# Gate rows of an MoE layer by a transposition and five DMA transfers instead of a matmul, and half of the additions of y moved behind the next first matmul group

## The chip, the cores and the metric

One core of one Trainium2 chip. The metric is device microseconds of one execution. Before the change the runs took 544.57, 544.6 and 544.8 us, the median is 544.6 us.

## What is computed

Sigmoid attention (4 batches of 448 tokens, 12 heads of 64), then a first mixture-of-experts layer with a skip, then a second one. Cut to the first layer, which is the one the change touches:

```python
def _moe_ref(x, w_skip, w_gate, w1, w2):        # x: 1792 tokens x 768
    do_compute = x @ w_skip > 0
    logits = xc @ w_gate                        # xc = x[do_compute], 8 experts
    e_idx = argmax(logits)
    gate_w = softmax(logits)[e_idx]             # one gate per token
    for e in range(8):
        h = maximum(xc[mask] @ w1[e], 0)        # 768 -> 1024
        y[mask] = gate_w[mask, None] * (h @ w2[e])
    out[do_compute] = xc + y
```

## The kernel before, in words

The activations stay on the chip transposed: `xT` holds 128 features by tokens, in six chunks. Attention runs over 12 duos of heads by 7 key blocks, 84 steps in all. Each step issues one group of score matmuls (L629), one sigmoid on ACT (L633), one group of value matmuls (L647) two steps behind, and then whatever small functions a table gives to that step (`late`, L671 to 687). When a duo ends, its two output banks are copied to `xT` by DVE (L554) and ACT (L552); the value matmuls of the next duo write the same two banks, so they wait for these copies.

Routing per batch finds the batch's most frequent expert. A batch in which more than 128 tokens choose one expert gets a dense pass (`dense`, L833): all 448 tokens go through that expert, with each input column multiplied by its gate beforehand, and zero for tokens that chose another expert. The multiplied input is made by `split_gated` (L734): for each of six chunks a product `xT * G` on DVE (L742), a rounded copy on ACT (L744) and the remainder on DVE (L745). `K["G"]` is the gate of each of the 448 tokens as a row, the same in all 128 partitions.

Before the change that row is made in two steps. `gate_cols` (L721) computes the gates as columns (`dense_gate`, L375: three DVE instructions, L380 to 384; 112 tokens by 4 columns) and writes four diagonal 112x112 blocks with them (L725). `gate_rows` (L729) multiplies a matrix of ones by these blocks on PE (L731), which sums each diagonal into a row in all partitions, and ACT copies the row back to `K["G"]` (L732).

This happens at two places in this execution:

- For the first dense batch, inside attention. `first_steps` (L753) gives a list of functions to the table at L698 to 701: the plan of the first dense batch (`plan_first`, L387, ending with `pa`, L402) and the rest of `gates` (L366 to 371) at g+7, `start` and `gate_cols` at g+8, `rows`, `piece(0)` and the deferred rest of `ranks` (L335 to 343) at g+12, and the next pieces one step later each. `start` reads the batch and expert numbers into registers and issues four weight loads of 768 KB on SP's queue (L506, L511). In the order of DVE the transposes of the next duo's k and q (L620) stand between `start` and `piece(0)`, the copies L554 stand between `piece(1)` and `piece(2)`. In the order of ACT the rounded copy of chunk 0 stands ahead of a sigmoid.
- For the second dense batch, in the second half of the first dense pass: `next_dense` (L1189), with `start` (two weight loads on SP and `gate_cols`) at sub-step 7.5 and `rows` at 10, where the sub-steps are those of `dense`.

After a dense pass `add_y` (L1239) adds the six banks of its output to `xT` on DVE (L1242). `block1` (L1280) runs one further dense pass; ahead of it `before()` does the sum of squares for the second layer's routing (L1151, L1153) and then `add_y` of the batch before. The relu of the first `h` group of the new pass needs ACT (L847) and then DVE (L848), behind these additions; the banks `YS` are written again only by the first `y` group.

All of this runs with an order written out by hand: each engine and each queue takes its instructions in the order of the program. `bank()` hands out two PSUM banks in turn.

Of the kernel before, what the change touches and what calls it, by code (L numbers as in the profile page):

```python
# [10 lines left out]
F32 = mybir.dt.float32  # L11
# [10 lines left out]
def sigmoid_attention_moe_moe_kernel(  # L22
# [15 lines left out]
    nc = tc.nc  # L38
# [40 lines left out]
    def const(name, shape, dt=F32):  # L79
        return cp.tile(shape, dt, tag=name, name=name)  # L80
# [10 lines left out]
    def setup_steps(tmp):  # L91
# [67 lines left out]
        def rest():  # L159
            K["desc"] = const("desc", [128, NE])  # L160
            nc.vector.tensor_scalar(K["desc"], K["io"][:, :NE], -1.0, float(NE), op0=ALU.mult, op1=ALU.add)
            K["gr"] = [const(f"gr{m}", [P, B, C, 2]) for m in range(2)]
            nc.vector.tensor_copy(K["gr"][0][:, :, :, 1], K["rid"])
            K["rest"] = const("rest", [128, B])
            K["pa"] = const("pa", [128, 4], I32)
            K["plan"] = const("plan", [128, 16])
            K["pb"] = const("pb", [128, 16], I32)
            K["G"] = const("G", [128, S])
            t = tmp.tile([128, 2, 9], F32, tag="seg_t", name="seg_t", bufs=1)
            a, z = t[:, 0, :8], t[:, 1, :8]  # L170
            K["seg"], K["off"] = const("seg", [128, 8]), const("off", [128, NK])
            nc.vector.tensor_scalar(a, K["io"][:, :8], -float(NK), K["pc"][:, 0:1], op0=ALU.mult, op1=ALU.add)
            nc.vector.tensor_single_scalar(z, a, float(NK), op=ALU.is_lt)
            nc.vector.scalar_tensor_tensor(K["seg"], a, 0.0, z, op0=ALU.is_ge, op1=ALU.mult)
            nc.vector.tensor_mul(a, a, K["seg"])
            nc.vector.reduce_sum(t[:, 0, 8:9], a, axis=AX.X)
            nc.vector.tensor_scalar(K["off"], K["io"][:, :NK], t[:, 0, 8:9], None, op0=ALU.is_equal)
# [179 lines left out]
    def gates(R, b0, b1):  # L357

        n = (b1 - b0) * C
        e = sm.tile([P, 2, (B - 1) * C, NE], F32, tag="ge", name="ge", bufs=1)  # L360
        s = sm.tile([P, B * C], F32, tag="gs", name="gs", bufs=1)
        sh = (R.SH[:, b0:b1] if R.m == 0 else R.SH).rearrange("p b c e -> p (b c) e")
        nc.scalar.activation(e[:, 0, :n], sh, AF.Sigmoid)
        nc.scalar.activation(e[:, 1, :n], sh, AF.Sigmoid, scale=-1.0)

        def rest():  # L366
            nc.vector.reciprocal(e[:, 1, :n], e[:, 1, :n])
            nc.vector.tensor_mul(e[:, 0, :n], e[:, 0, :n], e[:, 1, :n])
            nc.vector.reduce_sum(s[:, :n], e[:, 0, :n], axis=AX.X)
            nc.vector.tensor_single_scalar(s[:, :n], s[:, :n], 1e-9, op=ALU.add)  # L370
            nc.vector.reciprocal(K["gr"][R.m][:, b0:b1, :, 0], s[:, :n].rearrange("p (b c) -> p b c", c=C))

        return rest
# [182 lines left out]
    def attention():  # L556


        with ExitStack() as a:
# [112 lines left out]
            for g in range(G + LAG):  # L672
                w, h = divmod(g, NH)
                if 0 < w < N - 2 and h == 0:
                    load_qk(w + 2)
                if g < G:
                    score(w, h)
                if w + 1 < N and 0 <= h - LAG < 4:
                    load_v(w + 1, h - LAG)
                if w + 1 < N and h in (3, 4):  # L680
                    turn(w + 1, "kq"[h - 3])
                for r in {LAG: (), LAG + 1: (LAG + 1, LAG)}.get(h, (LAG,)):
                    if g >= r:
                        av(*divmod(g - r, NH))
                for f in [todo.pop(0)] if todo and g >= 2 else late.get(g, ()):
                    if f:
                        f()
                done = g - LAG + 1
                if done % NH == 0 and done > 0:
                    b, d = duos[done // NH - 1]  # L690
                    if d == NP // 2 - 1 and b < B - 1:
                        assert not todo
                        s1, s2, s3 = route_stages(R1, b, x_of(b))
                        todo = [None, s1, s2]
                        if b == B - 2:
                            ge = []
                            fs = [
                                s1, s2, lambda: ge.append(ranks(R1, 0, B - 1)), lambda: ge.append(gates(R1, 0, B - 1)), lambda: [plan_first(R1), ge[1]()],  # L698
                            ] + first_steps() + [lambda: ge[0]()]
                            at = [g + i for i in (2, 3, 5, 5, 7, 8, 8, 12, 12, 13, 14, 15, 16, 17, 18, 12)]  # L700
                            todo, late = [], schedule({}, fs, at)
            return ST[N - 1, "o"]

# [14 lines left out]

        return [piece(p) for p in range(ND)]

    def gate_cols(R, b):  # L721

        g = dense_gate(R, b)
        for c in range(C):
            nc.vector.tensor_scalar(  # L725
                K["G"][:P, c * P : (c + 1) * P], ident[:P, :P], g[:, c : c + 1], None, op0=ALU.mult
            )

    def gate_rows(ps):  # L729

        nc.tensor.matmul(ps[:, :S], lhsT=K["one"][:P], rhs=K["G"][:P], start=True, stop=True)  # L731
        nc.scalar.activation(K["G"], ps[:, :S], AF.Copy)  # L732

    def split_gated(xs, b):  # L734

# [17 lines left out]
    def first_steps():  # L753

        box = {}

        def start():
            pa = K["pa"]
            b = FIRST["b"] = nc.values_load(pa[0:1, 1:2], engines=XENG, min_val=0, max_val=B - 1)
            FIRST["e"] = nc.values_load(pa[0:1, 2:3], engines=[ENG.SP], min_val=0, max_val=NE - 1)  # L760
            load_unit(w1, w2, FIRST["e"], 0)
            load_unit(w1, w2, FIRST["e"], 1)
            box["p"] = split_gated(XST[0], b)

        def rows():
            gate_rows(bank("ps_G"))

        def piece(i):
            box["p"](i)
            if i == ND - 3:  # L770
                likely("none")
            if i == ND - 2:
                FIRST["n"] = nc.values_load(K["pa"][0:1, 0:1], min_val=0, max_val=1)

        return [start, lambda: gate_cols(R1, FIRST["b"]), rows] + [lambda i=i: piece(i) for i in range(ND + 1)]

    last_x = attention()

# [101 lines left out]
    def at_subs(ks, fs):  # L880
        return merge(*({k: f} for k, f in zip(ks, fs)))
# [307 lines left out]
    def next_dense(j):  # L1189

        box = {}
        xs = XST[(j + 1) % 2]

        def start():
            box["b"], box["e"] = rest_regs(j)
            load1(w1, box["e"], 0)
            load2(w2, box["e"], 0)
            gate_cols(R1, box["b"])

        def rows():  # L1200
            gate_rows(bank("ps_G"))
            box["p"] = split_gated(xs, box["b"])
            for p in range(2):
                box["p"](p)

        def last():
            load_unit(w1, w2, box["e"], 1)
            for f in split_unit(0)[:3]:
                f()

        return {
            7.5: start, 10: rows, 11: lambda: [box["p"](p) for p in (2, 3)], 12: lambda: [box["p"](p) for p in (4, 5, 6)], 13: last,
            14: lambda: [f() for f in split_unit(0)[3:]],
        }
# [21 lines left out]

        return sub

    def add_y(b):  # L1239
        for c in range(ND):  # L1240
            xd = batch_cols(c, b)
            nc.vector.tensor_add(xd, xd, YS[c][:, :S])  # L1242

    def start2(split):

# [31 lines left out]
                run(enumerated(route2_steps(0, XST[1])))  # L1277
            run(enumerated(start2(True)))

    def block1(j, before):  # L1280

        b, e = rest_regs(j - 1)
        xs = XST[j % 2]

        def r2():
            if j > 1:
                return {}
            f = route2_steps(0, XST[0])
            return at_subs((1, 4, 6, 2, 2.5, 5, 6, 8), f[:3] + f[6:])

        def general():
            with tc.If(count(R1) > 0) as cmp:
# [26 lines left out]
        with tc.If(nc.values_load(R1.LI[0:1, n : n + 1], min_val=0, max_val=NL[0]) < 1, label=f"one{j}") as cmp:  # L1319
            if j == B - 1:  # L1320
                general()
            else:
                with tc.If(NB["n"] > j) as more:
                    before()
                    dense(xs, beside(units1(e, 3), merge(r2(), next_dense(j), {13: lambda: likely(f"one{j + 1}")})))
                    block1(j + 1, lambda: add_y(b))
                with more.Else():
                    general()
        with cmp.Else():
# [35 lines left out]
    with cmp.Else():  # L1365
# [12 lines left out]
        with cmp2.Else():  # L1378
            steps = merge(
                next_dense(0), item_steps(R1, (9, 11, 12)),  # L1380
                {12: lambda: raw(batch_of(0)), 13: lambda: likely("one1"), 15: squares},
            )
            dense(XST[0], beside(units1(e), steps), NF // 2)
            block1(1, lambda: [squares_sum(), add_y(b)])


    e = expert_of(0)
# [226 lines left out]
```

## Time and profile before

| | |
|---|---|
| median of 3 runs | 544.6 us (544.57 to 544.8) |
| profiled execution, its own time | 543.8 us |
| its span, first to last instruction | 542.0 us |
| PE busy | 534.7 us (99%) |
| DVE busy | 297.4 us (55%) |
| ACT busy | 249.2 us (46%) |
| mean granted clock of TensorE | 0.999 |

Times in the rows below are microseconds from the start of the span. The profile names an instruction by engine, line and tiles; PE are matmuls, PEld weight loads of PE, SPq and ACTq the DMA issues of SP and ACT. A bracket at the end of a line is the time in which the engine stood idle before it, and what ended that time.

### The profile page before, as it was taken

The numbers are of one execution on the slowest core, as the hardware profiler recorded it, in microseconds if no ns is written. First come the engines' busy times: TensorE is split into PE (matmuls) and PEld (weight loads), VectorE is DVE, ScalarE is ACT, GpSimd is POOL, SyncE is SP. The second block draws the span as 40 slices with busy tenths as digits, with TensorE's granted clock in tenths as the row PEclk, the third lists the DMA queues.
The fourth block names the chain that finished last, engine by engine and source line by source line (L and its number), as shares of the span: only waits on it lengthen the run. The fifth ranks groups of instructions, "written<-read, shape, count | busy, mean of one in ns | idle before, by whom it ended". The sixth has DMA issues, their size and how long they took to land.

```text
span 542.0 us, 9985 instructions
## 1 busy us (share of the span) xinstructions
PE 534.7 (99%) x3601; PEld 420.6 (78%) x3601; DVE 297.4 (55%) x782; ACT 249.2 (46%) x408; POOL 56.1 (10%) x135
## 2 busy tenths in 40 slices
PE   8999999999999999999999999999999999999996
PEld 5464644535489899899869898999899999999984
DVE  3733243237877686774138677595566545462314
ACT  5766776767943355322209463165332333141210
POOL 5010000000000000265000000040004000403202
PEclk9999999999999999999999999999999999999999
DMA  9868666774461513315637206329234832384346
GB/s 176 152 116 147 118 113 114 128 127 115 169 191 49 177 59 122 115 61 166 245 118 278 70 4 231 117 51 263 81 116 111 224 111 66 122 177 161 115 145 194
DMA packets 172512, 73.35 MB, mean 135 GB/s; under 512 B 138162, under 2 KB 164102, under 8 KB 172432
## 3 DMA queue, kind: packets, MB, share of 16 engines
q1 hardware_dynamic: 150000, 65.94, 45.7%
q10 hardware_dynamic: 22064, 5.97, 4.7%
q0 software_dynamic: 368, 0.53, 0.5%
q8 instruction: 32, 0.52, 0.4%
q14 instruction: 48, 0.39, 0.2%
HBM read 66.90 MB, written 5.60 MB: 134 GB/s over the span
## 4 chain that ended last, share of the span: by engine, by line
PE 89%; DVE 4%; issue 3%; ACT 2%; DMA 1%; DVEq 0%; ACTq 0%
PE psO L647 12%; PE psS L629 11%; PE y L827 10%; PE bank L827 10%; PE y L829 10%; PE y L828 10%; PE bank L829 10%; PE bank L828 10%; PE bank L1011 2%; PE y L1036 1%; PE bank L250 1%; DMA k<-in_k_dram 1%; PE ps_r L250 1%; DVE l L813 1%; DVE xg L742 0%
## 5 line engine op out<-in xcount | busy, mean ns | idle before, releaser
L847 ACT ACTIVATE hh<-bank 128x448 fp32r<-128x448 f32 x48 | 26.1, 543 | 188.5 <-PE bank L829 167.1
L827 PE MATMUL y<-hh,h 128*128 128x448 f32 x288 | 107.3, 373 | 0.0
L827 PE MATMUL bank<-xs,h 128*128 128x448 f32 x288 | 106.5, 370 | 0.0
L829 PE MATMUL y<-hh,l 128*128 128x448 f32 x288 | 105.5, 366 | 0.0
L828 PE MATMUL y<-hl,h 128*128 128x448 f32 x288 | 105.5, 366 | 0.0
L829 PE MATMUL bank<-xs,l 128*128 128x448 f32 x288 | 105.4, 366 | 0.0
L828 PE MATMUL bank<-xs,h 128*128 128x448 f32 x288 | 105.3, 366 | 0.0
L633 ACT ACTIVATE A<-psS,bias 128x896 f32<-128x896 f32 x84 | 83.4, 1006 | 33.0 <-PE psS L629 32.1
L848 DVE SCALAR_TENSOR_TENSOR hl<-bank,hh 128x448 fp32r<-128x448 f32 x48 | 29.8, 621 | 121.0 <-ACT hh L847 118.0
L813 DVE TENSOR_TENSOR l<-r,h 128x512 fp32r<-128x512 f32 (+3 forms) x119 | 87.7, 788 | 3.0 <-ACT h L812 1.7
L629 PE MATMUL psS<-qT,kT 64*64 64x448 f32 x672 | 88.6, 541 | 0.6 <-ACT A L633 0.3
L647 PE MATMUL psO<-A,v 64*64 64x448 f32 x672 | 88.4, 539 | 0.0
L812 ACT ACTIVATE h<-r 128x512 fp32r<-128x512 f32 (+3 forms) x119 | 74.7, 691 | 0.1
L647 PEld LDWEIGHTS psO<-A,v 64*64 64x64 f32 x672 | 35.8, 133 | 32.6 <-issue 19.7
L827 PEld LDWEIGHTS bank<-xs,h 128*128 128x128 f32 x288 | 54.1, 188 | 8.1 <-issue 1.8
L827 PEld LDWEIGHTS y<-hh,h 128*128 128x128 f32 x288 | 54.1, 188 | 5.6 <-issue 1.2
L829 PEld LDWEIGHTS y<-hh,l 128*128 128x128 f32 x288 | 54.1, 188 | 4.8
L828 PEld LDWEIGHTS y<-hl,h 128*128 128x128 f32 x288 | 54.1, 188 | 4.8 <-issue 0.2
L829 PEld LDWEIGHTS bank<-xs,l 128*128 128x128 f32 x288 | 54.1, 188 | 4.5
L828 PEld LDWEIGHTS bank<-xs,h 128*128 128x128 f32 x288 | 54.1, 188 | 4.4
L629 PEld LDWEIGHTS psS<-qT,kT 64*64 64x64 f32 x672 | 33.2, 132 | 30.6 <-issue 15.7
L1421 POOL TENSOR_TENSOR row<-stg,gtt 128x448 f32<-128x448 f32 x20 | 19.1, 986 | 225.2 <-DVE stg L1414 171.9
(274 smaller groups left out, 395.8 us busy)
## 6 DMA issues: line engine op xcount, KB each, us to landing
r<-in_moe_w_dram SPq DMA_DIRECT2D x62, 768.0 KB, 4.7
k<-in_k_dram SPq DMA_DIRECT2D x44, 112.0 KB, 2.9
q<-in_q_dram SPq DMA_DIRECT2D x44, 112.0 KB, 3.4
v<-in_v_dram ACTq DMA_DIRECT2D x44, 112.0 KB, 2.9
out_dram<-row SPq DMA_DIRECT2D x12, 336.0 KB, 5.6
stg<-in_moe_w_dram SPq DMA_DIRECT2D x1, 768.0 KB, 7.6
row<-in_moe_w_dram SPq DMA_DIRECT2D x1, 768.0 KB, 8.7
out_dram<-row SPq DMA_DIRECT2D x5, 112.0 KB, 3.6
```

The source lines that it names most:

```text
L250: nc.tensor.matmul(ps[q : q + 32, :w], lhsT=lhsT, rhs=tokens(rhs, h), start=first, stop=last)
L629: nc.tensor.matmul(ps[KT * i : KT * i + KT, j, :S], lhsT=kT[r, i, h * KT : (h + 1) * KT], rhs=qT[r, i], start=True, stop=True,)
L633: nc.scalar.activation(at, ps[:, :, :S], AF.Sigmoid, bias=bias, scale=1.0 / math.sqrt(D))
L647: nc.tensor.matmul(ST[w, "o"][i][D * j : D * j + D, :S], lhsT=t[r, j, h, :], rhs=at[r, j, :], start=h == 0, stop=h == NH - 1,)
L812: nc.scalar.activation(dst_h, src, AF.Copy)
L813: nc.vector.tensor_sub(dst_l, src, dst_h.bitcast(F32))
L827: nc.tensor.matmul(ps, lhsT=ah, rhs=bh, start=first, stop=False)
L828: nc.tensor.matmul(ps, lhsT=ah, rhs=bl, start=False, stop=False)
L829: nc.tensor.matmul(ps, lhsT=al, rhs=bh, start=False, stop=last)
L847: nc.scalar.activation(a, ps[:, :S], AF.Relu)
L848: nc.vector.scalar_tensor_tensor(l, ps[:, :S], 0.0, a.bitcast(F32), op0=ALU.max, op1=ALU.subtract)
L1421: engine.tensor_tensor(ready(d0, d1)[:, :, d - d0], TURNED[:, d], gt.unsqueeze(2).to_broadcast([128, NK, 32]), op=ALU.mult)
```

## The change

`gate_cols` and `gate_rows` are replaced by `gate_row`: the gates go into a zeroed 128x32 block, one DVE transposition turns 32x32 blocks of it, four transfers on SP's queue write the four rows of 112 gates to a small buffer in DRAM (each as four pieces of 128 bytes), and a fifth transfer reads them back into all 128 partitions (512 pieces of 448 bytes, 224 KB). The fifth must wait until the four have landed. `gate_row` stands in `start`, ahead of the weight loads on the same queue. The first reciprocal of `gates` is issued with the sigmoids and no longer with the rest. `add_y` is cut in two: three chunks where all six stood, three at sub-step -0.5 of the next dense pass, behind the relu of its first `h` group.

```diff
@@ setup
-            K["G"] = const("G", [128, S])
             t = tmp.tile([128, 2, 9], F32, tag="seg_t", name="seg_t", bufs=1)
             a, z = t[:, 0, :8], t[:, 1, :8]
             K["seg"], K["off"] = const("seg", [128, 8]), const("off", [128, NK])
+            K["G"] = const("G", [128, S])
@@ gates
         nc.scalar.activation(e[:, 1, :n], sh, AF.Sigmoid, scale=-1.0)
+        nc.vector.reciprocal(e[:, 1, :n], e[:, 1, :n])
 
         def rest():
-            nc.vector.reciprocal(e[:, 1, :n], e[:, 1, :n])
@@ attention
-                            at = [g + i for i in (2, 3, 5, 5, 7, 8, 8, 12, 12, 13, 14, 15, 16, 17, 18, 12)]
+                            at = [g + i for i in (2, 3, 5, 5, 7, 8, 12, 13, 14, 15, 16, 17, 18, 12)]
@@ gate_cols and gate_rows go, gate_row comes
-    def gate_cols(R, b):
-
-        g = dense_gate(R, b)
+    GROW = tc.dram_tile([C, 128], F32, name="grow")
+
+    def gate_row(R, b):
+
+        t = sm.tile([128, 2, 1, NE, C], F32, tag="tt", name="gt").rearrange("p a o e c -> p a (o e c)")
+        nc.vector.memset(t[:, 0], 0.0)
+        dense_gate(R, b, t[:P, 0, :C])
+        nc.vector.transpose(t[:, 1], t[:, 0])
+        turned = t[:, 1].rearrange("(q z) r -> z q r", z=32)
         for c in range(C):
-            nc.vector.tensor_scalar(
-                K["G"][:P, c * P : (c + 1) * P], ident[:P, :P], g[:, c : c + 1], None, op0=ALU.mult
-            )
-
-    def gate_rows(ps):
-
-        nc.tensor.matmul(ps[:, :S], lhsT=K["one"][:P], rhs=K["G"][:P], start=True, stop=True)
-        nc.scalar.activation(K["G"], ps[:, :S], AF.Copy)
+            nc.sync.dma_start(GROW[c].rearrange("(q r) -> q r", r=32), turned[c])
+        row = GROW[:, :P].unsqueeze(0).to_broadcast([128, C, P])
+        nc.sync.dma_start(K["G"].rearrange("p (c x) -> p c x", c=C), row)
@@ first_steps
             FIRST["e"] = nc.values_load(pa[0:1, 2:3], engines=[ENG.SP], min_val=0, max_val=NE - 1)
+            gate_row(R1, b)
             load_unit(w1, w2, FIRST["e"], 0)
...
-        def rows():
-            gate_rows(bank("ps_G"))
...
-        return [start, lambda: gate_cols(R1, FIRST["b"]), rows] + [lambda i=i: piece(i) for i in range(ND + 1)]
+        return [start] + [lambda i=i: piece(i) for i in range(ND + 1)]
@@ next_dense
             box["b"], box["e"] = rest_regs(j)
+            gate_row(R1, box["b"])
+            bank("")
             load1(w1, box["e"], 0)
             load2(w2, box["e"], 0)
-            gate_cols(R1, box["b"])
 
         def rows():
-            gate_rows(bank("ps_G"))
             box["p"] = split_gated(xs, box["b"])
@@ add_y
-    def add_y(b):
-        for c in range(ND):
+    def add_y(b, chunks=range(ND)):
+        for c in chunks:
...
+    def halves_of_y(b):
+        return [lambda c=c: add_y(b, range(c, c + ND // 2)) for c in (0, ND // 2)]
@@ block1
-    def block1(j, before):
+    def block1(j, before, after):
...
-                return {}
+                return {-0.5: after}
             f = route2_steps(0, XST[0])
-            return at_subs((1, 4, 6, 2, 2.5, 5, 6, 8), f[:3] + f[6:])
+            return merge({-0.5: after}, at_subs((1, 4, 6, 2, 2.5, 5, 6, 8), f[:3] + f[6:]))
...
-                    block1(j + 1, lambda: add_y(b))
+                    block1(j + 1, *halves_of_y(b))
...
-            block1(1, lambda: [squares_sum(), add_y(b)])
+            block1(1, lambda: [squares_sum(), halves_of_y(b)[0]()], halves_of_y(b)[1])
```

## Rows read from the trace of the kernel before

**Rows 1.** The page: 40 equal slices, busy tenths of PE and its granted clock.

```profile
PE   8999999999999999999999999999999999999996
...
PEclk9999999999999999999999999999999999999999
```

**Rows 2.** Timeline, PE in attention around the gate matmul: start, duration, engine, line, operation.

```profile
132.67 1.12 PE L647 MATMUL psO<-A,v 64*64 64x448 f32 x8
...
133.72 1.02 PE L731 MATMUL ps_G<-G,one 112*128 112x448 f32 x2
...
134.88 0.98 PE L629 MATMUL psS<-qT,kT 64*64 64x448 f32 x8
```

**Rows 3.** Timeline of PE's weight loads at the change of duo.

```profile
139.46 0.20 PEld L647 LDWEIGHTS psO<-A,v 64*64 64x64 f32 x6 [0.62 <-DVE xT L554]
140.25 0.21 PEld L647 LDWEIGHTS psO<-A,v 64*64 64x64 f32 x8 [0.59 <-DMA v<-in_v_dram]
```

**Rows 4.** Timeline of DVE, 126 to 136 us.

```profile
126.05 1.26 DVE L554 COPY xT<-psO 64x448 f32<-64x448 f32 x2 [0.79 <-PE psO L647]
...
128.84 0.75 DVE L367 RECIPROCAL ge<-ge 112x96 f32<-112x96 f32 x1
...
131.22 0.21 DVE L380 TENSOR_TENSOR dgt<-OH,PRIM 112x32 f32 x1 [0.58 <-issue]
...
131.88 0.84 DVE L725 TENSOR_SCALAR G<-ident,dg 112x112 f32<-112x112 f32 x4
...
133.66 1.07 DVE L620 STREAM_TRANSPOSE qT<-q 128x896 f32<-128x896 f32 x1
135.35 0.63 DVE L742 TENSOR_TENSOR xg<-xT,G 128x448 f32<-128x448 f32 x1 [0.62 <-ACT G L732]
```

**Rows 5.** Groups by line: the only 128x32 transposition on DVE (count, busy us, mean ns).

```profile
L475 DVE STREAM_TRANSPOSE sel<-sel 128x32 f32<-128x32 f32 x2 | 0.4, 212 | 0.1
```

**Rows 6.** Timeline of SP and ACT: the first weight load, and its first reader.

```profile
130.51 0.43 SPq L506 DMA_DIRECT2D r<-in_moe_w_dram  x1
...
146.73 1.66 ACT L812 ACTIVATE h<-r 128x512 fp32r<-128x512 f32 x3
```

**Rows 7.** One line (L582): issue of k, ns min/median/max, and time to landing.

```profile
L582 SPq DMA_DIRECT2D k<-in_k_dram x44: 311/522/1873, 1.7 to 115.9; - x44
...
DMA to landing us min/median/max: 2.1/3.2/8.1
```

**Rows 8.** DMA issues: KB of each, median us to landing; the second is the last store.

```profile
r<-in_moe_w_dram SPq DMA_DIRECT2D x62, 768.0 KB, 4.7
...
out_dram<-row SPq DMA_DIRECT2D x1, 112.0 KB, 2.3
```

**Rows 9.** Timeline of PE around the second gate matmul.

```profile
186.78 0.36 PE L829 MATMUL bank<-xs,l 128*128 128x448 f32 x1
...
186.98 0.92 PE L731 MATMUL bank<-G,one 112*128 112x448 f32 x2
...
187.94 0.37 PE L828 MATMUL y<-hl,h 128*128 128x448 f32 x1
```

**Rows 10.** Timeline of DVE and ACT around the second gate row.

```profile
182.54 0.17 DVE L384 TENSOR_TENSOR dg<-dg,gr 112x4 f32<-112x4 f32 x1
...
190.28 1.16 DVE L742 TENSOR_TENSOR xg<-xT,G 128x448 f32<-128x448 f32 x2
...
201.87 1.66 ACT L812 ACTIVATE h<-r 128x512 fp32r<-128x512 f32 x3
```

**Rows 11.** Timeline of DVE at the additions of y.

```profile
213.71 3.27 DVE L1242 TENSOR_TENSOR xT<-xT,y 128x448 f32 x6
216.90 0.61 DVE L848 SCALAR_TENSOR_TENSOR hl<-bank,hh 128x448 fp32r<-128x448 f32 x1
```

**Rows 12.** Timeline of PE at the same place.

```profile
216.98 0.37 PE L829 MATMUL bank<-xs,l 128*128 128x448 f32 x1
217.57 0.96 PE L250 MATMUL bank<-stg,wr 128*32 128x224 f32 x16 [0.22 <-DVE hl L848]
```

## The prediction

> **What bounds the kernel now.** First the page's slices: PE is busy nine tenths or more in all of them but the first and the last, at the full granted clock of 2.4 GHz [rows 1]. PE works off one long list, so a microsecond taken off that list, or off a wait of PE, is gained unless a later wait gives it back, and a new wait of PE is lost in full. Then PE's timeline at the places that the change touches.
>
> In attention the value group at 132.67 takes 0.75 us like its neighbours, so the next score group could start at 133.42. It starts at 134.88, behind the two gate matmuls [rows 2]. At the change of duo the value matmuls start at 139.46, when DVE's copies of the old duo are done, and wait once more for the last load of v [rows 3]. The DVE timeline shows what leads there: the gates from 131.22, the transpose of q until 134.73, the first product with G at 135.35 [rows 4]. From that product DVE runs through to the end of the copies: product 0, the four instructions left from `ranks`, product 1, remainder 0, two copies. So 139.46 lies 4.1 us behind it. This distance carries the argument.
>
> **Attention: what goes, what comes.** On PE the two matmuls go, 1.46 us by the rows (134.88 less 133.42); on ACT the copy L732. On DVE the reciprocal of 0.75 us moves to just ahead of the copies of 126.05, where DVE idled 0.79 us, so it costs nothing there and the gates start at 130.47 instead of 131.22; without that idle time it would be a move of 0.75 us and no gain [rows 4]. The three gate instructions keep their 0.66 us (131.22 to 131.88), the four diagonal blocks (0.84) go. The zeroing has no row; it lies between 0 and the 0.21 of a transposition of the same 128x32 size [rows 5], and I take 0.15, nearest to that row. With the transposition the block is ready at 130.47 + 0.15 + 0.66 + 0.21 = 131.5. The transposes of k and q follow 1.2 us earlier than before, so score matmuls can start at 133.5.
>
> The row is now waited for in a new way. SP was free at 130.51 [rows 6], so it waits for the block, and with it the four weight loads queued behind `gate_row`. A hand-over between engines I put at 0.1 us. Four issues at 0.31 (the shortest of L582) to 0.52 (the median) [rows 7]; I take 0.4, as these have few pieces, and the fourth starts at 131.5 + 0.1 + 1.2 = 132.8. Nothing as small as 512 bytes is in the trace. The last store takes 2.3 us for 112 KB, and 768 KB take 4.7 [rows 8], which makes 3.7 us per MB and a fixed 1.9; the fastest load of 112 KB took 2.1 [rows 7], 1.7 without its bytes. The ends are 1.2 and 2.3, I take 1.7, by the fastest load, since the queues are nearly empty then. So the rows are in DRAM at 134.5, and after another 0.1 the fifth transfer is issued. It moves 224 KB: between the 2.1 of the fastest 112 KB and the 3.2 of the median one [rows 7], taken as 2.3, near the fast end, because its pieces of 448 bytes are larger and fewer than those loads'. G then arrives at 134.6 + 2.3 = **136.9**, with ends of 131.5 + 0.1 + 0.9 + 1.2 + 0.1 + 2.1 = 135.9 and 131.5 + 0.1 + 1.6 + 2.3 + 0.1 + 3.2 = 138.8.
>
> The Trainium skill's page "DMA: Bandwidth & Descriptors", section "Anatomy of one DMA — SWDGE (gpsimd) path", speaks against two dependent small transfers: it gives about 2.0 us of fixed time to each, most of it the receipt of the write, heaviest for HBM. By its 2.0 us and 436 GB/s, an estimate from that page, G would arrive at 137.4 and the sum below be 0.5 us larger; the last store's 2.3 us agrees with it, the fastest load's 2.1 is a little below.
>
> Before, the product started at 135.35. It is 1.55 us later now, and as DVE takes its instructions in order, the copies behind it and the value matmuls on PE are as late: 141.0 instead of 139.46. ACT is held too, since the rounded copy of chunk 0 stands ahead of a sigmoid, but that sigmoid is done by about 139.1 and does not end last. The 1.46 us that PE gained are thus given back in this wait, and 1.55 lost: **+1.55**. Part returns: the wait of 0.59 for v [rows 3] came with v loads sharing the DMA engines with 3 MB of weights, which now start after 134.6. PE overlapped part of that wait, so the gain lies between 0 and 0.59; I take **-0.3**. The four weight loads start about 4.5 us later; four times 768 KB at 3.7 us per MB are 11 us, ending near 146.5, while the first reader is at 146.73 [rows 6] and needs only the first. Costs nothing; without that cover each microsecond of delay would be one of PE.
>
> **The second row.** The two gate matmuls stand between 186.78 and 187.94, where two ordinary steps of 0.2 us (186.78 to 186.98) would have led to 187.18 [rows 9]: **-0.76**. The row hides here. The gates end at 182.7; with zeroing and transposition the block is at 183.1, and the same 5.4 us put G at 188.5. Its first product was at 190.28 [rows 10], in DVE order behind other work. At the far end of 7.3 us G comes at 190.4, about no loss. The two weight loads behind it on SP start near 187 and are first needed at 201.87 [rows 10].
>
> **The additions.** Six take 3.27 us ahead of the relu's second half (L848) [rows 11], and PE's routing matmuls, which reuse its bank, wait for it: 217.57 after 216.98 [rows 12]. Three fewer end it 1.6 us earlier, so the wait goes: between the 0.22 shown as idle and the 0.4 beyond a usual step; **-0.3**. The three moved ones take the DVE time that the relu's half left, ahead of the weight remainders, which start when they did. The y banks are rewritten only behind the 1.6 us of routing matmuls. This also takes up the shift of PE by the second row.
>
> **Sum.** 1.55 - 0.3 - 0.76 - 0.3 = +0.2 us on the profiled execution's 543.8, so 544.0. The median of the runs lies 0.8 above it: **544.8**. In general the sum is G's arrival less 136.7. About 0.2% (1.09 us) is what a measurement here can tell from no change, so the arrival has to be below 135.6 for faster and above 137.8 for slower.
>
> **Rivals.**
> - The transfers are quick. At the short ends (135.9) the sum is -0.8. With 0.4 less still, and the whole 0.59 of the v wait, it is -1.5: 543.1. For it: the queues are nearly empty. Against: no row below 2.1 us. Chance 0.17.
> - The transfers are slow, and the wait for G takes more than the matmuls gave. Issues of 0.52 and landings of 2.3 and 3.2 put G at 138.8: +2.1, 546.7. It decides from 137.8 on. For it: the median loads, and a v load running on ACT's queue at that moment. Chance 0.22.
> - The gains outside attention don't come, as DVE is nearly as full as PE between the two places: +0.2 + 0.76 + 0.3 = +1.3, 545.9. Against: PE has no idle row there. Chance 0.05.
> - PE's idle time costs clock. It would stand still about 2.5 us, in two holes between 137 and 141. Some 7.5 us of matmuls follow in attention; at 1.2 GHz they would take up to 7.5 more: 545 to 552. Against: the first slice has PE at eight tenths, over 1.3 us idle, at the full clock [rows 1]. The Trainium skill, "TensorE: Matmul & The Clock Gate", Part 1, states that an idle PE falls to 1.2 GHz; the rows here show no fall. Chance 0.03.
>
> The forecast, no change that can be told, has 0.53.
>
> **How the numbers follow.** Faster 0.17, same 0.53, slower 0.22 + 0.05 + 0.03 = 0.30. The likeliest case's own range is 543.7 to 545.7. From 543.4 to 546.8 it takes in the short ends and the slow transfers at their far end, and leaves out the quickest and the clock.
>
> **What would show it.** Right: the broadcast into G landing at 136 to 138 with DVE idle ahead of L742 for about 3 us, PE's value matmuls waiting for DVE's copies until 140 to 142, no gate matmul near 187, and no DVE wait ahead of the routing matmuls of the next pass. Wrong: G before 135.6 or after 138; DVE waiting for G at the second place; a wait for weights; a granted clock below full in attention.

## The result and the profile after

The changed kernel is slower: a median of 552.8 us (551.24 to 552.96, 4 runs) against 544.7 (544.57 to 544.86, 4 runs) of the kernel before, a ratio of 1.0142 [1.013, 1.0154]. The prediction was 544.8 with 546.8 as its upper end. The profiled execution has a span of 551.2 us, 9.2 more than before.

First the page of the changed kernel: the same two slices as [rows 1].

```profile
span 551.2 us, 9988 instructions
...
PE   8999999999699999999999999999999999899996
...
PEclk9999999999899999999999999999999999899999
```

Two slices between the first and the last now stand out, with less of PE and of the clock: the eleventh (138 to 152 us), in attention, and the thirty-fifth (469 to 482), far behind every line of the diff. The windows say how much clock was lost (columns: window, its length, then busy us and instructions of PE, PEld, DVE, ACT, POOL; granted clock; DMA share; GB/s):

```profile
136.00:140.00 4.00, 2.32 (x28) 0.83 (x19) 0.06 (x1) 0.43 (x1) 0.00 (x0) 1.00 0.56 158
140.00:143.90 3.90, 0.98 (x8) 0.21 (x8) 3.67 (x10) 3.20 (x6) 0.00 (x0) 0.97 1.01 371
143.90:147.00 3.10, 3.06 (x19) 1.07 (x23) 3.03 (x6) 2.75 (x4) 0.00 (x0) 0.50 1.06 389
147.00:150.00 3.00, 3.00 (x36) 1.19 (x32) 1.37 (x3) 1.87 (x3) 0.00 (x0) 0.98 0.11 42
478.20:481.60 3.40, 3.40 (x10) 2.99 (x10) 0.00 (x0) 0.00 (x0) 0.58 (x1) 0.50 0.51 90
481.60:485.00 3.40, 3.40 (x18) 3.12 (x17) 0.76 (x2) 1.40 (x3) 0.00 (x0) 1.00 1.03 176
```

Now the timeline of PE after (the lines of the dense matmuls are L826 to L828 here, one less than before):

```profile
137.35 0.98 PE L629 MATMUL psS<-qT,kT 64*64 64x448 f32 x8
142.12 0.98 PE L629 MATMUL psS<-qT,kT 64*64 64x448 f32 x8 [3.80 <-ACT A L633]
143.94 3.27 PE L647 MATMUL psO<-A,v 64*64 64x448 f32 x16 [0.83 <-DVE xT L554]
146.98 0.98 PE L629 MATMUL psS<-qT,kT 64*64 64x448 f32 x8
...
153.15 0.47 PE L826 MATMUL bank<-xs,h 128*128 128x448 f32 x1
...
221.97 0.96 PE L250 MATMUL bank<-stg,wr 128*32 128x224 f32 x16 [0.16 <-DVE hl L847]
...
228.27 0.40 PE L267 MATMUL bank<-ident,xg 128*112 128x128 f32 x2 [0.73 <-DVE hl L847]
...
475.25 0.37 PE L828 MATMUL y<-hh,l 128*128 128x448 f32 x1
477.93 0.55 PE L826 MATMUL bank<-xs,h 128*128 128x448 f32 x1 [2.31 <-issue]
```

And three starts on PE before that answer to these; none of them was among the earlier rows:

```profile
147.91 0.47 PE L827 MATMUL bank<-xs,h 128*128 128x448 f32 x1
...
224.00 0.45 PE L827 MATMUL bank<-xs,h 128*128 128x448 f32 x1
...
470.25 0.36 PE L827 MATMUL bank<-xs,h 128*128 128x448 f32 x1
```

Laid side by side, start by start, PE in the kernel after is later by:

| place | later by, us | new there |
|---|---|---|
| attention ahead of the changed lines (as DVE's copies: 126.05, now 126.81) | 0.76 | 0.76, from the start-up; this differs from run to run |
| first dense pass (147.91, now 153.15) | 5.24 | **+4.48, attention** |
| 187 to 191, second gate row | 4.42 | -0.82, the two gate matmuls |
| 224.00, now 229.32 | 5.32 | +0.9, all of it given back |
| last dense pass (470.25, now 477.93) | 7.68 | **+2.47, a stall with no wait** |
| 4 us behind that stall (472.28, now 481.63) | 9.35 | **+1.67** |
| end of the span | 9.2 | -0.2 |

PE has the same 0.76 from 14 us on up to the change. About 0.1 us comes back between 224 and 470.

**Attention.** DVE's timeline after, the answer to [rows 4] and [rows 11]; L743 is the first product with G, L726 to L728 build the block, L847 is the relu's second half, L1241 the additions:

```profile
126.81 1.26 DVE L554 COPY xT<-psO 64x448 f32<-64x448 f32 x2
...
131.08 0.09 DVE L726 MEMSET gt<- 128x32 f32 x1 [0.46 <-issue]
...
131.89 0.21 DVE L728 STREAM_TRANSPOSE gt<-gt 128x32 f32<-128x32 f32 x1
...
133.10 1.07 DVE L620 STREAM_TRANSPOSE qT<-q 128x896 f32<-128x896 f32 x1
139.94 0.62 DVE L743 TENSOR_TENSOR xg<-xT,G 128x448 f32<-128x448 f32 x1 [5.77 <-DMA G<-grow]
...
142.61 1.27 DVE L554 COPY xT<-psO 64x448 f32<-64x448 f32 x2
...
188.16 0.21 DVE L728 STREAM_TRANSPOSE gt<-gt 128x32 f32<-128x32 f32 x1
...
196.02 1.16 DVE L743 TENSOR_TENSOR xg<-xT,G 128x448 f32<-128x448 f32 x2 [0.41 <-DMA G<-grow]
...
219.71 1.68 DVE L1241 TENSOR_TENSOR xT<-xT,y 128x448 f32 x3
221.30 0.62 DVE L847 SCALAR_TENSOR_TENSOR hl<-bank,hh 128x448 fp32r<-128x448 f32 x1
221.84 1.67 DVE L1241 TENSOR_TENSOR xT<-xT,y 128x448 f32 x3
...
227.50 0.62 DVE L847 SCALAR_TENSOR_TENSOR hl<-bank,hh 128x448 fp32r<-128x448 f32 x1
```

SP's timeline, the four writes, the read, and the first weight load queued behind them:

```profile
132.13 2.42 SPq L731 DMA_DIRECT2D grow<-gt  x4
135.83 0.41 SPq L733 DMA_DIRECT2D G<-grow  x1
136.45 1.17 SPq L506 DMA_DIRECT2D r<-in_moe_w_dram  x1
```

From the finished block (131.89 + 0.21 = 132.10) to the product at 139.94 pass 7.8 us. Four issues take 2.42, some 0.6 each; the read goes out 1.28 later, and its 224 KB have landed 4.1 us after that. DVE stands still for 5.77 us and PE for 3.80 (the first hole ends with ACT's sigmoid behind the held rounded copy, the second, of 0.83, with DVE's copies). Then comes a second loss: the 16 value matmuls take 3.04 us (143.94 to 146.98), at a granted clock of 0.50, which is 1.2 GHz.

**The stall at 477.9.** PE waits there for nothing that the profile names. The branch `label="single"`, ahead of the last dense pass, has this row on PE's queue, one instruction, after and then before:

```profile
L1572 PEldq COMPARE_BRANCH  x1: 5700/5700/5700, 472.2 to 472.2; - x1
```

```profile
L1570 PEldq COMPARE_BRANCH  x1: 335/335/335, 467.0 to 467.0; - x1
```

PE's queue runs about 3 us ahead of its array (467.0 against 470.25 before), so 0.335 us are hidden. 5.7 are not: 472.2 + 5.7 = 477.9, where PE starts again. Behind it the granted clock is 0.50, that is 1.2 GHz, from 478.2 to 481.6, and full again from there.

### The profile page after: what moved, and what is told of

It is laid out like the page before. It is cut to its first block, busy times and chain, and to the rows that moved or that the text cites. A ratio compares the mean times of both kernels' runs of the same rounds, so it can differ in the third digit from the quotient of the medians.

```text
span 551.2 us, 9988 instructions
## 1 busy us (share of the span) xinstructions
PE 536.6 (97%) x3597; PEld 422.0 (77%) x3597; DVE 296.1 (54%) x778; ACT 248.7 (45%) x406; POOL 56.0 (10%) x135
## 4 chain that ended last, share of the span: by engine, by line
PE 87%; DVE 5%; issue 3%; DMA 2%; ACT 1%; SPq 0%; DVEq 0%; ACTq 0%; POOL 0%; POOLq 0%
PE psO L647 11%; PE psS L629 11%; PE bank L826 10%; PE bank L828 10%; PE bank L827 10%; PE y L826 10%; PE y L828 9%; PE y L827 9%; DMA G<-grow 2%; PE bank L1010 1%; PE y L1035 1%; PE bank L250 1%; DVE l L812 1%; PE busy L665 1%; PE ps_r L250 1%
## 5 line engine op out<-in xcount | busy, mean ns | idle before, releaser
L826 PE MATMUL bank<-xs,h 128*128 128x448 f32 x288 | 107.3, 373 | 2.3 <-issue 2.3
L826 PE MATMUL y<-hh,h 128*128 128x448 f32 x288 | 107.0, 372 | 0.0
L828 PE MATMUL bank<-xs,l 128*128 128x448 f32 x288 | 106.1, 368 | 0.0
L828 PE MATMUL y<-hh,l 128*128 128x448 f32 x288 | 105.5, 366 | 0.0
L847 DVE SCALAR_TENSOR_TENSOR hl<-bank,hh 128x448 fp32r<-128x448 f32 x48 | 29.8, 622 | 125.1 <-ACT hh L846 121.9
L826 PEld LDWEIGHTS bank<-xs,h 128*128 128x128 f32 x288 | 54.6, 189 | 10.8 <-issue 4.4
L826 PEld LDWEIGHTS y<-hh,h 128*128 128x128 f32 x288 | 54.2, 188 | 5.3 <-issue 1.0
L828 PEld LDWEIGHTS bank<-xs,l 128*128 128x128 f32 x288 | 54.5, 189 | 4.6
L828 PEld LDWEIGHTS y<-hh,l 128*128 128x128 f32 x288 | 54.1, 188 | 4.6
```

The source lines that it names most:

```text
L826: nc.tensor.matmul(ps, lhsT=ah, rhs=bh, start=first, stop=False)
L828: nc.tensor.matmul(ps, lhsT=al, rhs=bh, start=False, stop=last)
L847: nc.vector.scalar_tensor_tensor(l, ps[:, :S], 0.0, a.bitcast(F32), op0=ALU.max, op1=ALU.subtract)
```

## The experiments

Three batches, each with the kernel before on the same chip: medians 544.19, 544.19 and 544.41 us. "Later" below means PE's start, side by side with the kernel before as in the table.

### The branch

**e1_code_shift.** Five matmuls added to the kernel after, inside the branch `none`, whose code this execution jumps over ("isn't taken" below): nothing that runs is changed, all PE code behind it lies 20 instructions further.

```diff
+        for _ in range(5):
+            nc.tensor.matmul(BANKS[0][:, :128], lhsT=K["one"][:P], rhs=K["one"][:P], start=True, stop=True)
         run(item_steps(R1, (0, 1, 2)))
```

> Theory: the 5.7 us that PE's branch at the last dense pass takes in the changed kernel (0.34 before), and the half clock behind it, hang on where PE's code lies, because the change took PE instructions out. This kernel runs the same instructions, with five matmuls more in a branch that is not taken, so only the code behind them lies elsewhere: the branch takes under 0.5 us again and about 4 us of the 8.1 come back (548.7 us). Rival: the branch is slow because of what runs at that moment (weight loads, a late hint); then nothing changes (552.8 us).

Measured: 547.92 us, ratio 1.0076 [1.0059, 1.0093].

```profile
L1574 PEldq COMPARE_BRANCH  x1: 336/336/336, 470.9 to 470.9; - x1
```

No stall at the last pass, and nothing is lost behind 230; attention still costs 4.22 (4.65 at the first dense pass, 0.43 of it from the start-up). So the stall belongs neither to the gates nor to the additions, but to where the code lies; from the ratios it is worth 0.66%, 3.6 us.

**e5_before_code_shift.** The kernel before, with routing transposes and some matmuls left out of the same branch, which isn't taken; the branch `single` comes to lie 22 PE instructions nearer to the start.

```diff
-            for j in range(C // 2):
+            for j in range(0 if DEAD[0] else C // 2):
```

> The kernel before, with five matmuls (20 PE instructions with their weight loads) left out of a branch that is not taken, so that PE's later code lies where the changed kernel has it; what runs is the same. Theory (the place of the code decides): PE's branch at the last dense pass takes some 5.7 us instead of 0.34, PE loses 2.5 us there and up to 1.7 more at half clock: 546.5 to 548.5 us against 544.4. Rival (something else of the change makes it slow, the place only helped by chance): 544.4 us as before.

Measured: 543.67 us, ratio 0.9992 [0.9982, 1.0002]; the branch keeps its 335 ns. A miss: the place aimed at was not reached. The compiled lists show it 6 instructions ahead of its place in the kernel after, so what follows is only that 6 instructions are enough.

**e9_before_no_hint and e10_after_no_hint.** The program marks the likely side of that branch, and PE's queue carries a prefetch hint for it, a row of its own at 281.7 in the kernel before. The kernels before and after without it:

```diff
-            todo = merge(todo, item_steps(R2, (9, 11, 13)), {13: lambda: likely("single")})
+            todo = merge(todo, item_steps(R2, (9, 11, 13)))
```

> The kernel before, with the hint for the branch labelled single left out. That branch stands ahead of the last dense pass of the second layer and takes 335 ns on PE's queue in the kernel before, 5700 in the kernel after. Theory (the 5.7 us are those of a jump for whose target the instructions were not fetched ahead; the hint normally hides them, and in the kernel after it did not): the branch takes 4 to 7 us, PE stands still about 2.3 us ahead of the last dense pass, part of the pass behind it runs at half clock, and the run is 3 to 5 us longer than before. Rival (the hint has no part in it): about 335 ns and the time of before.

> The kernel after, with the same hint left out. Theory (the hint did nothing there): branch about 5700 ns and 552.8 us, as after with the hint. Rival (the hint brought the instructions of the wrong place or still shortened the wait): clearly longer or shorter than 5700 ns, and the time moves by more than 1 us.

Measured: before without the hint 548.21 us, ratio 1.0079 [1.0057, 1.0101]; after without it 552.95, 1.0157 [1.0117, 1.0196], the same as with it within its interval. The branch's row in the first, and PE behind it:

```profile
L1570 PEldq COMPARE_BRANCH  x1: 5856/5856/5856, 466.3 to 466.3; - x1
```

```profile
472.23 0.65 PE L827 MATMUL bank<-xs,h 128*128 128x448 f32 x1 [2.49 <-issue]
```

This is the stall of the kernel after, in the kernel before: 2.65 later at the last pass and 1.65 behind it. In the kernel after, without the hint, the branch takes 5336 ns. The hint was there and brought nothing.

The times of e10 and of the kernel after are alike, their profiles are not quite. In e10 the half clock in attention lasts until 150.8, and attention costs 6.45 us; behind its stall of 1.94 us the clock stays full. In e3 (below) too the clock is 1.00 behind a stall of 2.33 us. So the loss of clock behind this stall came in three of the five profiles that have it (after, e9, e12).

**e11_one_matmul and e12_sixtyfour_matmuls.** As e1, with 1 and 64 matmuls (`range(1)`, `range(64)`).

> The kernel after with one matmul more in the branch that is not taken, where five brought the branch from 5700 to 336 ns. It moves all code behind by 4 PE instructions, one further than the kernel with the attention of before had it, which took 1757 ns. If the duration follows from where the code of the branch lies: 335 to 1757 ns, and a time near 548 to 549.5. If it is the number of executed instructions or the data that decides: 5700 ns and 552.8, since neither changes.

> The kernel after with 64 matmuls in the branch that is not taken, which moves the code behind by 256 PE instructions, 16 KB. If the place counts by its remainder within a block of 16 KB or a fraction of it: 5700 ns again, and 552.8 us. If any move away from the old place is enough: some 336 ns and 547.9 us, as with five matmuls. Branches ahead may change too, as the not taken code lies before all but the first.

Measured: 548.28 us, 1.0066 [1.0033, 1.01], and 551.23, 1.0125 [1.009, 1.016]. Their rows of the branch, one matmul and then sixty-four:

```profile
L1574 PEldq COMPARE_BRANCH  x1: 2017/2017/2017, 472.1 to 472.1; - x1
```

```profile
L1574 PEldq COMPARE_BRANCH  x1: 5680/5680/5680, 470.1 to 470.1; - x1
```

The 2017 ns of e11 lie just above the range that was expected, its time within it; neither 2017 nor e2's 1757 ns holds PE up. A move by 256 instructions brings the full stall back. The kernels with the hint together, by the place of the branch among PE's instructions, counted in the compiled lists from its place in the kernel after:

| place | kernels, ns of the branch |
|---|---|
| -6 | e5 335 |
| 0 | after 5700, e3 5720 |
| +3 | e2 1757 |
| +4 | e11 2017 |
| +16 | before 335 |
| +19, +20 | e7 336; e1 336, e8 336 |
| +40 | e4 361 |
| +256 | e12 5680 |

So the hint fails at 0, helps in part at +3 and +4 and works at -6 and from +16 to +40, and the bad place comes again after 256 instructions, or a fraction of that. Which fraction stays open.

What the branch waits for can be read from the traces. They hold the single transfers of the queue that the page calls instruction (q8: 31 of 0.51 MB in all in the kernel after, 16 KB each). Over all fourteen traces the rows of PE's branches divide in two. Each of the 12 that take over 0.5 us ends 1.3 to 1.6 us behind the end of such a transfer: in the kernel after one runs from 475.53 to 476.52, and the branch ends at 477.87; in e2 and e11 it had started 0.80 and 0.55 us ahead of the branch, and the row is the shorter for it. Ahead of the 44 quick rows (402 ns at most) the last transfer had ended 3.4 us or more before the branch did (462.63 against 467.30 in the kernel before). By all that these traces show, the slow rows are a wait for code. Why the hint has not brought it in time at these places stays open.

### Attention

**e4_busy_in_wait.** The kernel after, with 20 transposes of the identity on PE, whose result nobody reads, at the point where PE waits for the late product.

```diff
+                if g == 79:
+                    fill = bank("fill")
+                    for _ in range(20):
+                        nc.tensor.transpose(fill[:, :128], ident, ident)
                 for f in [todo.pop(0)] if todo and g >= 2 else late.get(g, ()):
```

> The changed kernel with 20 transposes of the identity on PE inside its wait for G, some 4 us of work whose output nobody reads. Theory: the wait stays, as it is DVE's, but the granted clock stays full, so the 16 value matmuls behind it take 1.5 and not 3.0 us: about 1.2 us less (551.6 us). Rival: the slow matmuls come from their inputs or from transfers running beside them; then they stay at 3 us and the time is the same or longer (552.8 us or more).

Measured: 554.38 us, ratio 1.0201 [1.0178, 1.0225], longer, not shorter. The place itself did what the clock theory says:

```profile
137.16 2.40 PE L688 MATMUL fill<-ident 128*128 128x128 f32 x20
141.58 0.98 PE L629 MATMUL psS<-qT,kT 64*64 64x448 f32 x8 [2.01 <-ACT A L633]
143.39 1.73 PE L647 MATMUL psO<-A,v 64*64 64x448 f32 x16 [0.83 <-DVE xT L554]
144.94 0.93 PE L629 MATMUL psS<-qT,kT 64*64 64x448 f32 x8
```

The 16 value matmuls take 1.55 us instead of 3.04: PE stood still for 2.01 and 0.83 us here and kept its clock, and for 3.80 and 0.83 in the kernel after and lost it. What made the run longer are branches again. All code behind the addition lies 40 instructions further, and while `single` is quick at 361 ns, `none` and `one1`, 392 and 350 ns before, now are as follows, each ending 1.4 to 1.6 us behind an instruction transfer:

```profile
L1360 PEldq COMPARE_BRANCH  x1: 3362/3362/3362, 150.1 to 150.1; - x1
...
L1325 PEldq COMPARE_BRANCH  x1: 4535/4535/4535, 213.9 to 213.9; - x1
```

**e3_pieces_later and e8_pieces_two_later.** The products with G put three and two steps later, behind the copies that PE waits for; e8 (14 to 20 in place of 15 to 21 below) with the five matmuls of e1 besides.

```diff
-(2, 3, 5, 5, 7, 8, 12, 13, 14, 15, 16, 17, 18, 12)
+(2, 3, 5, 5, 7, 8, 15, 16, 17, 18, 19, 20, 21, 12)
```

> The changed kernel with the six pieces of the first gated input three steps later, so that DVE's copies of the old duo stand ahead of the first product with G. Theory: PE's value matmuls no longer wait for G, the 3.7 us and the half clock go and the 1.3 us of the two matmuls stay gained in attention; its end comes about 5.5 us earlier than in the changed kernel, less what the late pieces hold up at the first dense pass (0 to 3 us): 547 to 550 with the slow branch. Rival: the weight loads behind G on SP's queue are what is late; then the first dense pass waits for them as before and under 1 us comes back.

> The changed kernel with the pieces two steps later (the first just behind the copies of the old duo) and with PE's later code at its old place by five matmuls in a branch that is not taken. Theory: no wait for G on PE, a shorter one than with three steps at the first dense pass, a fast branch: the first dense pass starts 0.5 to 1.3 us earlier than in the kernel before, the rest is even: 543.2 to 544.0 us. Rival: the sigmoid behind the first rounded copy on ACT now waits for G, and holds the scores: 545 us or more.

Measured: e3 549.52 us, ratio 1.0113 [1.0088, 1.0137], with the slow branch (5720 ns) in it; e8 543.67 us, 0.9989 [0.9978, 1.0]. DVE and PE in e3:

```profile
139.11 1.16 DVE L743 TENSOR_TENSOR xg<-xT,G 128x448 f32<-128x448 f32 x2 [1.20 <-DMA G<-grow]
```

```profile
136.43 1.73 PE L629 MATMUL psS<-qT,kT 64*64 64x448 f32 x16
137.97 1.74 PE L647 MATMUL psO<-A,v 64*64 64x448 f32 x16
...
147.56 0.47 PE L826 MATMUL bank<-xs,h 128*128 128x448 f32 x1 [1.84 <-ACT h L811]
```

G comes as late as ever and DVE waits for it, but nothing that PE needs stands behind. PE runs on at full clock; in e3 the first dense pass starts 0.2 earlier than before and in e8 0.2 later, start-up left out. The 0.5 to 1.3 us that e8 was expected to gain there did not come, though its time lies in the expected range. The 1.46 us of the two gate matmuls are not gained even so, since the chain through the last products now ends last (the wait of 1.84 for ACT). e8 is even with the kernel before, or ahead by up to 0.2%; e5, which runs nothing other than the kernel before, measured 0.9992, so this is no gain that can be told.

**e2_attention_as_before.** The first gate row by matmuls as in the kernel before, the second by transfers, the additions as after (with `gate_cols` and `gate_rows` put back and the step list of before).

```diff
-            gate_row(R1, b)
             load_unit(w1, w2, FIRST["e"], 0)
...
+        return [start, lambda: gate_cols(R1, FIRST["b"]), rows] + [lambda i=i: piece(i) for i in range(ND + 1)]
```

> The first gate row is made by the diagonal blocks and PE again, the second by transfers, the additions stay split. Theory (the wait for G in attention costs 3.7 us on PE and the half clock behind it 0.8 more): attention is 4.5 us shorter than in the changed kernel, its end is as in the kernel before, and the second place and the additions together change under 0.3 us; 548.3 us if PE's branch at the last pass stays slow, 544.3 if that goes as well, since PE's code lies elsewhere again. Rival: the change of the second place or of the additions has a part in the loss; then 549 or more with the branch as slow as it was.

Measured: 544.08 us, ratio 0.9998 [0.9988, 1.0008]. With attention undone (and the branch at 1757 ns, which costs PE nothing) no loss is left, and no gain.

### The second row and the additions

**e7_second_row_alone and e6_split_additions_alone.** e7 is e2 with the six additions whole (and four matmuls in the branch that isn't taken); e6 is the kernel before with the split additions of the change.

```diff
-            block1(1, lambda: [squares_sum(), halves_of_y(b)[0]()], halves_of_y(b)[1])
+            block1(1, lambda: [squares_sum(), add_y(b)], lambda: None)
```

> Only the second gate row is made by transfers; the first is made on PE, the additions stand whole, and the place of PE's later code is kept. Theory (DVE, not PE, sets the pace from the second row to the next pass): PE gains 0.8 us at the second row and gives it all back, and more than with split additions, at the routing matmuls of the next pass, since DVE comes 0.5 us or more later there: 0 to +0.8 us on PE's list by then (544.4 to 545.2 us). Rival: the gain stays and the split had cost it: 543.6 us.

> The kernel before with the additions of y split and nothing else. Theory: the routing matmuls of the next pass no longer wait for the relu's second half, and DVE is early enough for the second one: 0.3 to 0.4 us less on PE's list, under what a run can tell (544.0 us). Rival: the split makes the wait of the transposes after the first y group (0.9 us in the changed kernel); then 0.5 us or more longer at that place.

Measured: e7 544.79 us, ratio 1.0008 [0.9996, 1.0021]; e6 543.94, 0.9992 [0.9981, 1.0002]. The routing matmuls behind the additions in e7 (with their wait; 0.22 in [rows 12]), and DVE at G:

```profile
218.08 0.96 PE L250 MATMUL bank<-stg,wr 128*32 128x224 f32 x16 [1.38 <-DVE hl L862]
```

```profile
190.91 1.16 DVE L756 TENSOR_TENSOR xg<-xT,G 128x448 f32<-128x448 f32 x2 [0.36 <-DMA G<-grow]
```

The second row alone takes 0.82 us off PE at 187 to 191 and gives back 1.16 at 218, where PE waits 1.38 us for DVE's half of the relu. DVE sets the pace there: its chain from the product with G runs 0.63 later than before (190.91 against 190.28) and ends 0.5 later. In e6 the wait of 0.22 at the same matmuls is gone and PE is 0.29 earlier, with nothing given back by 224.

## Why the prediction was wrong

**The block.** Right: 131.5 was said; 132.10 less the 0.76 of start-up is 131.3. The reciprocal hid behind DVE's idle time as argued.

**G's arrival, the step that the sum hung on.** Wrong: 5.4 us from the block were said, 7.8 measured, beyond the far end of 7.3. The four issues were taken at 0.4 us and took 0.6 (+0.5 over the four and the hand-over); the write's landing at 1.7 was about right (+0.1); the read was taken at 2.3, by the fastest 112 KB load, and took 4.1 (+1.8). It moves twice the bytes of that load, and its 4.0 us from issue to landing lie above the 3.2 of the median load, which was the far end; at the second place the first reader starts 4.4 us after the issue, and in e7 the landing takes 4.3. Two rows of the kernel before answer to this and were passed over: loads of the same 224 KB, and a transfer of 512 bytes, of which the prediction says that the trace has none.

```profile
k<-in_k_dram SPq DMA_DIRECT2D x2, 224.0 KB, 4.3
...
itau<-in_moe_tau_dram POOLq DMA_DIRECT2D x1, 0.5 KB, 5.5
```

The near end of 1.2 for the write had no row behind it. With the measured arrival, 139.94 - 0.76 = 139.2, the prediction's own sum gives 139.2 - 136.7 = +2.5, or 547.1: slower, and just above the range, but far from 552.8. The rival of slow transfers, given 0.22, named this term. The estimate from the Trainium skill's "DMA: Bandwidth & Descriptors", "Anatomy of one DMA — SWDGE (gpsimd) path", was a total of 5.9 us from the block, nearer but short as well: by its 2.0 us and 436 GB/s the read would be 2.5, and the measurement decides. That section is on transfers issued by GpSimd, and these go out on SP's queue. Whether the read is slow from its 448-byte pieces or from the weight loads issued right behind it (SP at 136.45) was not tried. The trace's single transfers say where the 4.0 us went: the first of the 512 pieces starts at 136.91, 1.1 us after the issue, 457 have started by 138.5, and the other 55, with pieces of the weights among them from 138 on, take until 139.53. So about 1 us of it may be the weights.

**From G to the value matmuls.** Right: 4.1 us were said, and 143.94 - 139.94 is 4.0. The 0.59 wait for v is gone, as hoped. So the value matmuls start 143.94 - 0.76 - 139.46 = 3.7 us later instead of 1.55, less 0.59 for v, where 0.3 was said.

**The clock.** The rival was given 0.03, because the first slice shows 1.3 us of idle time at the full clock. It happened: two holes of 3.80 and 0.83 us, then 0.50 of the clock for 3.1 us, 3.04 - 1.55 = 1.5 us by e4's row. 3.7 - 0.6 + 1.5 = 4.6, and 4.48 were measured. The Trainium skill, "TensorE: Matmul & The Clock Gate", Part 1, says that an idle PE falls to 1.2 GHz, and the trace after agrees: 0.50 from 143.90 to 147.00. The argument against it failed because it weighed 1.3 us of idle time against a forecast of 2.5, and the holes became 4.6. It also trusted the page's 9 in the first slice. PE's rows there, the first two before and the third after, show something else:

```profile
1.35 3.25 PE L665 MATMUL busy<-ident 128*128 128x128 f32 x14 [1.35 <-POOL ident masks.py:199]
...
5.53 0.71 PE L665 MATMUL busy<-ident 128*128 128x128 f32 x5
```

```profile
5.89 1.27 PE L665 MATMUL busy<-ident 128*128 128x128 f32 x5
```

Fourteen transposes of the identity in 3.25 us, where e4's twenty take 2.40, are about half the pace, right behind idle time. In the kernel after the slow pace lasts longer (1.27 us for five instead of 0.71), and this makes up the start-up difference of the table.

**The second row, -0.76.** The matmuls went and took 0.82 with them. That the row hides was wrong: from the block (188.16 + 0.21) to the product it is 7.65 us, with DVE waiting 0.41 for it. The larger error is the step that PE's list is what ends here: in [rows 12] PE already waits 0.22 for DVE, so 0.82 less on PE's list is a longer wait. The rival "the gains outside attention don't come, as DVE is nearly as full as PE", given 0.05, is what e7 shows.

**The additions, -0.3.** Right alone: -0.29 in e6. In the kernel after the wait at the routing matmuls stays at 0.16, since PE comes there 0.8 earlier by the second row. The step that the moved three "take the DVE time that the relu's half left" failed: the next half (L847) comes at 227.50, and the routing transposes wait 0.73 for it. Together the two parts outside attention come to about nothing in the kernel after and in e2 (+0.1 and +0.2 from the first dense pass to 224); in e1, e10, e11 and e12 0.4 to 0.75 us stays gained, and why it does there was not followed.

**What was not in the prediction at all** is the branch: 2.47 + 1.66 us of span. No row near the diff could show it, and the 335 ns on PE's queue in the kernel before give no sign of it; e9 shows what the hint hides there.

The account by the two profiles: of 9.2 us of span 0.76 are start-up, 4.48 attention (1.25 forecast), 0.1 the second row and the additions (-1.06 forecast), 2.47 and 1.67 the branch (not forecast), and 0.3 comes back on the way. By ratios: 1.42% is 7.7 us. e1, without the stall, has 0.76%, 4.1 us, near its attention's 4.22; the other 3.6 is the branch.

## What to carry to other kernels

A value that goes to DRAM and comes back as a broadcast has a latency of its own (7.8 us here, 7.65 at the second place) that no single transfer's median shows; price its parts by rows of the same size where the trace has them, and put its readers behind everything that another engine waits for, as in e3 and e8, before the matmuls that it replaces are taken out. A hole in PE's work costs its length and can cost clock behind it, 1.5 us here; filling it with transposes that nobody reads kept the clock in e4. And before a difference of some microseconds is put down to an edit, compare the rows of the branches on PE's queue in both kernels: a few unused instructions ahead of them can add or remove some 4 us.

## What was not expected of the hardware

- The same branch with the same hint takes 335 ns or 5.7 us, by where its code lies: 5700 at the place of the kernel after, 335 six instructions earlier, 1757 and 2017 three and four later, 5680 again 256 later. Without a hint it takes 5336 and 5856.
- PE's branch goes on 1.3 to 1.6 us after a 16 KB transfer of instructions has ended, in all 12 slow rows of fourteen traces.
- Behind that stall of 2.3 us the clock falls too (0.50 from 478.2 to 481.6), so that it costs 4.1 us in all; in e3 and e10 it did not fall behind 2.33 and 1.94 us.
- A read of 224 KB from DRAM, broadcast in 448-byte pieces, lands in 4.0 us (4.3 in e7), while 768 KB of weights take 4.6 in the median.
